# One burst per mixed step: weighted queries behind the x transpose, query transposes last, sums held back

## The chip, the cores and the metric

The kernel runs on one core of a Trainium2 chip. The metric is the device time of one execution in microseconds (us), lower is better. The engines work through instruction queues of their own: TensorE (PE, matmuls and transposes), VectorE (DVE), ScalarE (ACT), GpSimd (POOL) and SyncE (SP), which issues the DMAs. PSUM is the memory that TensorE writes, SBUF the one that holds everything else on chip.

## What is computed

Linear attention with exponential random features (8 batches, 8 heads, 576 rows, head size 64, 128 features), and a gated MLP on its result:

```python
def phi(x):                                   # x scaled by 64 ** -0.25
    h = x @ omega.T - sum(x * x) / 2          # omega: 128 x 64
    return exp(h - max(h)) / sqrt(128)
kv = phi(k).T @ v                             # 128 x 64 for a head
z = sum of phi(k) over the rows
attn = (phi(q) @ kv) / (phi(q) @ z + 1e-6)
x = attn as 4608 x 512                        # tokens x (heads * 64)
g = x @ w_gate                                # 512 x 1536
out = (g * sigmoid(g) * (x @ w_val)) @ w_out  # float32
```

The weights arrive as 64-bit numbers and are turned into float32 on the chip.

## The kernel before

**Two streams on one TensorE.** The attention runs in steps; each step takes two groups of 256 rows of two heads (a q and a k group in the mixed steps, two k groups in the first six). The MLP is a generator, `stream`, that goes over tiles of 512 tokens: gates `g` (L659, `mm1`), their Silu (L733), values `v` (L659), the product `sl` (L752) which is split in a high and a low part `hh`, `hl` (L755, L756), and the outputs `o` (L668, `mm2`). Every product is three matmuls, high by high, high by low and low by high; MLP matmuls have 512 columns. The last four tiles go in two pairs (`pair_rounds`), with seven products of combined operands in the place of eight; the sums of the products are made by `plus` (L971, DVE) and by ACT copies, the combined operands of the next pair (`t3`, `t1`, `t2`, `t4`, eight subtractions) by `next_x` (L829, DVE).

**What sets the order.** The code is recorded by the framework's list scheduler, which keeps a priority by the order of the code and puts every engine's instructions in a fixed row. The main loop calls, for each step n, the functions of a tuple in turn. `CLOSE` is for the early steps (to about 140 us), `GROUPED` for the rest: there the attention's functions stand together in a burst, and six `SHARE`s follow, each of which lets `stream` run for a share of the time that step n is given. `convert_all` (L268 to L280) turns one weight block after another into float32, one operation at a time between the shares: ACT Abs L268, DVE L270 to L278, POOL L280; in this profile it ends at about 427 us.

**A mixed step's parts.** `st_transpose` (PE `pt` L385, ACT copy `x` L393), `st_project` (PE `pp` L408, 16 matmuls), `st_max` (DVE L419 to L429), `st_exp` (ACT `ph` L440), `k_accumulate` (PE `kvacc` L542, two halves of a step, two steps later). When a half of a batch's heads is complete, `kv_finalize` copies `kvacc` to `kvr` (ACT L456).

For batches 0 to 3 a q group goes this way: `q_transpose` (PE `ptq` L566, ACT copy `qt` L568), a step later `q_mult` (PE `po` L583, eight 65-column matmuls; DVE `dn` L590, reciprocal L591, `xn` L593), a step later `q_out` (PE `xt` L616, then ACT and DVE to the MLP's `xh`, `xl`, or ACT `xo` L638 and a DMA to DRAM). For batches 4 to 7 the denominators are made before: `kv_finalize` also transposes the row of z (PE `zp` L462, ACT `zs` L464, DMA `zd` L466), `load_z` reads it back to all partitions (DMA `zt` L478), POOL multiplies (`jk` L502), DVE sums, POOL normalises `ph` (`q_norm`, L518); then `ptq` L566 and `xt` L623.

**PSUM.** `ps_moe` has three banks (`g`, `v`, `o`), `ps_proj` two (`pp`), and one bank each have `ps_tr` (`pt`, and `xt` from the mixed steps on), `kvacc`, and `ps_att`, which `po`, `ptq` and `zp` share: whoever of them comes next waits until the one before it has been read, `po` by DVE `xn`, `ptq` by ACT `qt`, `zp` by ACT `zs`.

Of the kernel before, what the change touches and what calls it, by code (L numbers as in the profile page):

```python
# [16 lines left out]
ALU = mybir.AluOpType  # L17
# [6 lines left out]
def kernel(  # L24
# [11 lines left out]
    nc = tc.nc  # L36
# [61 lines left out]
    def ps_att(name, shape):  # L98
        return ps_a.tile(shape, F32, name=name, tag="b")
# [30 lines left out]
    def slots(n, kind):  # L130

        if not 0 <= n < NS:
            return []
        return [(i, b, g, (kgroups if kd == "k" else qgroups)[g]) for i, (kd, b, g) in enumerate(steps[n]) if kd == kind]

    def pairs_of(gr):
        return [(2 * c, 2 * c + 1) for c in range(CH)] if gr is None else [gr[:1]] * CH
# [315 lines left out]
    def kv_finalize(b, a2):  # L453
        acc = kvacc.pop((b, a2))
        raw = att.tile([P, 4, VW], F32, name=f"kvr{b}_{a2}", tag="kvr", bufs=4)
        nc.scalar.copy(raw, acc)  # L456
        for j in range(2):
            kvst[b, 2 * a2 + j] = raw[:, 2 * j : 2 * j + 2, :]
        if b >= BPOOL:

            zp = ps_att(f"zp{b}_{a2}", [4, P])
            nc.tensor.transpose(zp, raw[:, :, D], ident)  # L462
            zs = att.tile([4, P], F32, name=f"zs{b}_{a2}", tag="zs")
            nc.scalar.copy(zs, zp)  # L464
            zd = dram.tile([4, P], F32, name=f"zd{b}_{a2}", tag="zd", bufs=4)
            nc.sync.dma_start(zd, zs)  # L466
            zds[b, a2] = zd

    zds = {}
    zbc = {}  # L470

    def load_z(n):

        for _, b, g, gr in slots(n, "q"):
            if g == 0 and b >= BPOOL:
                zt = att.tile([P, 2, 4, M], F32, name=f"zt{b}", tag="zt")
                for a2 in range(2):
                    nc.sync.dma_start(  # L478
                        zt[:, a2], zds.pop((b, a2)).rearrange("(o h) m -> o h m", o=1).broadcast_to([P, 4, M])
                    )  # L480
                    zbc[b, a2] = zt[:, a2]
# [42 lines left out]
    def k_accumulate(n, half):  # L524

        n -= KLAG
        ks = [(b, g, gr, c) for _, b, g, gr in slots(n, "k") for c in range(CH)]
        for b, g, gr, c in ks[half * len(ks) // 2 : (half + 1) * len(ks) // 2]:
            ph, vt = box["k", b, g], vrows[b, g]
            if c == CH - 1:  # L530
                busy.remove(vt)
                del box["k", b, g]
            for j, pr in enumerate(pairs_of(gr)[c]):
                a2 = pr // 2
                first = (b, a2) not in kvacc
                if first:
                    kvacc[b, a2] = ps_k.tile([P, 4, VW], F32, name=f"kvacc{b}_{a2}", tag="kv")
                acc = kvacc[b, a2]
                done.setdefault((b, a2), []).append(pr)
                last = LAST[pr] == (g, c)  # L540
                for hh in range(2):
                    nc.tensor.matmul(  # L542
                        acc[:, 2 * (pr % 2) + hh, :],
                        ph[:, c, hh * M : (hh + 1) * M],
                        vt[:, 2 * c + j if gr is None else c, hh, :],
                        start=first and hh == 0,
                        stop=last,
                        skip_group_check=True,
                    )
                if len(done[b, a2]) == NACC:  # L550
                    kv_finalize(b, a2)
        return bool(slots(n, "k"))
# [236 lines left out]
    sevens = {}  # L789

    factors, ahead = {}, {}

    def first_x():

# [26 lines left out]
    def next_x(r):  # L821

        for half, names in ((0, ("b11", "t1")), (1, ("b21", "b22"))):
            for j, name in zip(PAIRS[r], names):
                nc.sync.dma_start(ahead[name], x_dram[j][:, half * CH : (half + 1) * CH, :])
        yield
        for o, a, b in (("t3", "b22", "t1"), ("t1", "t1", "b11"), ("t2", "b22", "t1"), ("t4", "b21", "t2")):
            for c in range(CH):
                nc.vector.tensor_tensor(ahead[o][:, c], ahead[a][:, c], ahead[b][:, c], op=ALU.subtract)  # L829
                yield  # L830

    def new_factors():
# [5 lines left out]
    def split_x(name):  # L838
        hi, lo = factors[name]
        nc.scalar.copy(hi, ahead[name])  # L840
        nc.vector.tensor_tensor(lo, ahead[name], hi.bitcast(F32), op=ALU.subtract)
# [27 lines left out]
    def product(ps, n, wts, start):  # L869
        (wh, wl), (xh, xl) = wts[PROD[n][0]], factors[PROD[n][1]]  # L870
        for c in range(CH):
            w_ = slice(c * P, (c + 1) * P)
            for m, (a_, b_) in enumerate(((wh, xh), (wh, xl), (wl, xh))):
                nc.tensor.matmul(  # L874
                    ps, a_[:, w_], b_[:, c, :],
                    start=start and c == 0 and m == 0, stop=c == CH - 1 and m == 2, skip_group_check=True,
                )
# [6 lines left out]
    def pair_rounds(todo):  # L884
# [51 lines left out]
        for vi, (r, k_, pf) in enumerate(pair_visits):  # L936
            unit = [0]
            then = pair_visits[vi + 1] if vi + 1 < len(pair_visits) else None
            new_x = then and then[0] != r
            if k_ == 1 and r + 1 < len(PAIRS):  # L940
                prep = next_x(r + 1)
            sl, h = {}, {}

            def gate(n, src_):

                nc.scalar.activation(sl[n], src_, AF.Silu)

            def value(n, src_):

                h[n] = hbuf[used[1] % len(hbuf)]  # L950
                used[1] += 1
                hh, hl = h[n]
                nc.vector.tensor_tensor(sl[n], src_, sl[n], op=ALU.mult)
                nc.scalar.copy(hh, sl[n])
                nc.gpsimd.tensor_tensor(hl, sl[n], hh.bitcast(F32), op=ALU.subtract)

            for i, use in ((0, gate), (1, value)):
                wts = sevens[i]
                if i == 0:
                    for n in range(4):  # L960
                        sl[n] = slbuf[used[0] % len(slbuf)]
                        used[0] += 1
                keep = {}

                def copy(name, ps):
                    keep[name] = kp[:, ("m1", "m5", "u2").index(name)]
                    nc.scalar.copy(keep[name], ps)

                def plus(n, ps, name):
                    o = sl[n] if i == 0 else kp[:, 3]  # L970
                    nc.vector.tensor_tensor(o, ps, keep[name], op=ALU.add)  # L971
                    use(n, o)

                a, c, d = (ps_w.tile([P, T], F32, name=f"{e}{vi}_{i}", tag="w") for e in "acd")
                for n in ORDER:
                    weights_work(vi, unit[0])
                    unit[0] += 1
                    product({5: c, 3: c, 2: d}.get(n, a), n, wts, n in (1, 5, 2))
                    if n == 1:
                        copy("m1", a)  # L980
                    elif n == 5:
                        copy("m5", c)
                    elif n == 6:
                        copy("u2", a)
                    elif n == 3:
                        plus(1, c, "u2")
                    elif n == 7:
                        plus(3, a, "m5")
                    elif n == 2:
                        plus(0, d, "m1")  # L990
                    else:
                        use(2, a)
                    if new_x and i == 1:
                        split_x(PROD[n][1])
                    yield US7
                    if n in (5, 3, 2, 4) and one_down():
                        yield MM2
            assert not todo
            wts2 = {f: weights[f, 2] for f in (2 * pf, 2 * pf + 1)}
            for j, o in ((PAIRS[r][1], 1), (PAIRS[r][0], 0)):  # L1000
                ht = {2 * pf + n: h[2 * n + o] for n in range(2)}
                todo += [(j, k_, ht, wts2, None, tt) for tt in range(T // P)]
# [7 lines left out]
    def give(us):  # L1010
# [28 lines left out]
    )  # L1039
    GROUPED = (  # L1040
        q_out,
        st_project,
        q_transpose,
        lambda n: k_accumulate(n, 0),
        lambda n: k_accumulate(n, 1),
        st_max,
        st_exp,
        q_den,
# [2 lines left out]
        SHARE,  # L1051
        SHARE,
        lambda n: q_norm(n + 1),
        q_mult,
        SHARE,
        SHARE,
        SHARE,
# [68 lines left out]
```

## Time and profile before

| | |
|---|---|
| time, median of 3 runs | 1218.34 us (1216.60 to 1220.92) |
| the profiled execution | 1219.54 us, of it span 1217.8 us, 1.7 us around it |
| PE busy, share of the span | 1173.9 us, 96% |
| ACT, DVE, POOL busy | 54%, 53%, 48% |
| mean granted TensorE clock | 0.987 of full speed |
| PE busy in 100 to 200, 200 to 300, 300 to 400, 400 to 500 us | 95.7, 95.6, 96.3, 94.5 |
| PE busy in 600 to 800, 800 to 900, 900 to 1000 us | 199.95, 94.3, 100 |
| DVE busy in 100 to 200, 200 to 300 us | 83.8, 50.8 |

Profile times count from the start of the span. A row of the timeline has start, duration, engine, line, operation, output and inputs, their shapes and the count of merged instructions; brackets hold the idle time of the engine ahead of it and what released it. MLP matmuls start 0.227 us apart at full clock, though the modelled duration shown is 0.39: spacing is what counts. A row of the waits has the total, the times and the longest.

### The profile page before, as it was taken

The numbers are of one execution on the slowest core, as the hardware profiler recorded it, in microseconds if no ns is written. First come the engines' busy times: TensorE is split into PE (matmuls) and PEld (weight loads), VectorE is DVE, ScalarE is ACT, GpSimd is POOL, SyncE is SP. The second block draws the span as 40 slices with busy tenths as digits, with TensorE's granted clock in tenths as the row PEclk, the third lists the DMA queues.
The fourth block names the chain that finished last, engine by engine and source line by source line (L and its number), as shares of the span: only waits on it lengthen the run. The fifth ranks groups of instructions, "written<-read, shape, count | busy, mean of one in ns | idle before, by whom it ended". The sixth has DMA issues, their size and how long they took to land.

```text
span 1217.8 us, 18846 instructions
## 1 busy us (share of the span) xinstructions
PE 1173.9 (96%) x6705; PEld 969.5 (80%) x6705; DVE 647.1 (53%) x1231; ACT 660.9 (54%) x1461; POOL 585.0 (48%) x500
## 2 busy tenths in 40 slices
PE   6999999999999999999999999999899999999998
PEld 5888887888787678878888877878688888888886
DVE  5588886364656763434333354174545456545544
ACT  4687866574465555466555666353454445454431
POOL 3343442254344645545454585444565553555541
PEclk9799999999999999999999999999999999999999
DMA  6556656253544433244222211334321111312103
GB/s 151 125 132 157 168 146 186 50 153 86 170 113 119 119 86 93 71 112 101 66 62 81 67 60 45 88 103 138 96 55 58 48 49 26 104 52 53 52 18 69
DMA packets 174109, 113.52 MB, mean 93 GB/s; under 512 B 125856, under 2 KB 144320, under 8 KB 174016
## 3 DMA queue, kind: packets, MB, share of 16 engines
q1 hardware_dynamic: 174016, 112.32, 34.1%
q8 instruction: 53, 0.87, 0.3%
q14 instruction: 40, 0.33, 0.1%
HBM read 87.10 MB, written 25.18 MB: 92 GB/s over the span
## 4 chain that ended last, share of the span: by engine, by line
PE 78%; DVE 8%; DMA 5%; POOL 3%; issue 3%; ACT 2%; SPq 1%; POOLq 0%; ACTq 0%; DVEq 0%
PE o L668 21%; PE g L659 11%; PE a L874 10%; PE v L659 10%; PE pp L408 5%; PE c L874 5%; PE kvacc L542 4%; PE ptq L566 3%; PE d L874 2%; PE pt L385 2%; DMA nat<-in_k_dram 2%; PE po L583 2%; PE xt L623 1%; DVE st L426 1%; SPq L343 1%
## 5 line engine op out<-in xcount | busy, mean ns | idle before, releaser
L440 ACT ACTIVATE ph<-pp,st 128x128 f32<-128x128 f32 x576 | 157.5, 390 | 32.8 <-DVE st L429 32.3
L697 DVE TENSOR_TENSOR acc<-o,acc 128x512 f32<-128x512 f32 x140 | 95.8, 685 | 100.5 <-PE o L668 100.3
L392 POOL TENSOR_TENSOR sq<-nat 128x512 f32<-128x512 f32 x72 | 77.2, 1072 | 120.1 <-DMA nat<-in_k_dram 98.7
L426 DVE TENSOR_REDUCE st<-pp 128x4 f32<-128x512 f32 x144 | 93.0, 683 | 68.0 <-PE pp L408 67.9
L251 POOL TENSOR_TENSOR wlo<-wraw,whi 128x512 fp32r<-128x512 f32 x76 | 99.9, 1325 | 55.5 <-ACT whi L250 55.2
L408 PE MATMUL pp<-omT,x 64*128 64x128 f32 x1152 | 97.4, 301 | 5.5 <-ACT x L393 4.5
L668 PE MATMUL o<-whi,hh 128*128 128x512 f32 x240 | 96.6, 402 | 6.3 <-ACT sl L733 3.4
L408 PEld LDWEIGHTS pp<-omT,x 64*128 64x128 f32 x1152 | 79.4, 199 | 24.1 <-issue 11.6
L756 POOL TENSOR_TENSOR hl<-sl,hh 128x512 fp32r<-128x512 f32 x60 | 78.8, 1318 | 37.5 <-ACT hh L755 37.4
L659 PE MATMUL g<-xh,whi 128*128 128x512 f32 x240 | 96.9, 404 | 0.0
L659 PE MATMUL v<-xh,whi 128*128 128x512 f32 x240 | 95.7, 399 | 0.7 <-DVE acc L697 0.7
L668 PE MATMUL o<-whi,hl 128*128 128x512 f32 x240 | 94.4, 393 | 0.9 <-POOL hl L756 0.9
L659 PE MATMUL g<-xl,whi 128*128 128x512 f32 x240 | 94.4, 393 | 0.0
L659 PE MATMUL g<-xh,wlo 128*128 128x512 f32 x240 | 94.4, 393 | 0.0
L668 PE MATMUL o<-wlo,hh 128*128 128x512 f32 x240 | 94.3, 393 | 0.0
L659 PE MATMUL v<-xh,wlo 128*128 128x512 f32 x240 | 93.7, 391 | 0.0
L659 PE MATMUL v<-xl,whi 128*128 128x512 f32 x240 | 93.6, 390 | 0.0
L502 POOL TENSOR_TENSOR jk<-ph,zt 128x512 f32<-128x512 f32 x32 | 41.3, 1295 | 107.0 <-ACT ph L440 106.9
L280 POOL TENSOR_TENSOR wc<-st,wc 128x512 f32<-128x512 f32 x36 | 48.7, 1355 | 90.4 <-DVE wc L278 43.8
L419 DVE TENSOR_REDUCE st<-sq 128x8 f32<-128x512 f32 x72 | 49.0, 681 | 80.6 <-POOL sq L392 80.6
L865 POOL TENSOR_TENSOR wlo<-s,whi 128x512 fp32r<-128x512 f32 x44 | 65.2, 1498 | 33.9 <-DVE late L971 12.1
L865 POOL TENSOR_TENSOR wlo<-wraw,whi 128x256 fp32r<-128x256 f32 (+1 forms) x44 | 45.6, 1036 | 72.9 <-ACT whi L864 72.3
(252 smaller groups left out, 2925.3 us busy)
## 6 DMA issues: line engine op xcount, KB each, us to landing
wraw<-wscr SPq DMA_DIRECT2D x120, 256.0 KB, 2.7
wscr<-wc SPq DMA_DIRECT2D x36, 256.0 KB, 2.4
out_dram<-acc SPq DMA_DIRECT2D x72, 128.0 KB, 2.3
nat<-in_k_dram SPq DMA_DIRECT2D x64, 128.0 KB, 2.9
v<-in_v_dram SPq DMA_DIRECT2D x64, 128.0 KB, 3.3
nat<-in_q_dram SPq DMA_DIRECT2D x64, 128.0 KB, 2.9
st<-in_moe_w_gate_dram SPq DMA_DIRECT2D x12, 512.0 KB, 4.4
st<-in_moe_w_val_dram SPq DMA_DIRECT2D x12, 512.0 KB, 4.9
```

Of the source, the lines that this page charges most:

```text
L251: nc.gpsimd.tensor_tensor(lo, raw, hi.bitcast(F32), op=ALU.subtract)
L392: nc.gpsimd.tensor_tensor(sq, nat, nat, op=ALU.mult)
L408: nc.tensor.matmul(pp[hh][:, i, c, :], x[r, i, c * P : (c + 1) * P], omT[r], start=True, stop=True)
L419: nc.vector.tensor_reduce(st[:, 0].rearrange("p i c h -> p (i c h)"), sq.rearrange("p i c h d -> p (i c h) d"), axis=AX.X, op=ALU.add,)
L426: nc.vector.tensor_reduce(st[:, 1, :, :, hh], pp[hh], axis=AX.X, op=ALU.max, negate=True)
L440: nc.scalar.activation(ph[:, c, hh * M : (hh + 1) * M], pp[hh][:, i, c, :], AF.Exp, bias=st[:, 3, i, c, hh : hh + 1], scale=1.0,)
L659: nc.tensor.matmul(ps, a_[:, ws], b_[:, c, :], start=n == 0, stop=n == 3 * NC - 1)
L668: nc.tensor.matmul(ps, a_[:, ts_], b_, start=first and n == 0, stop=last and n == 2)
L697: nc.vector.tensor_tensor(a_, po, a_, op=ALU.add)
L756: nc.gpsimd.tensor_tensor(hl, h, hh.bitcast(F32), op=ALU.subtract)
L865: nc.gpsimd.tensor_tensor(lo, src_, hi.bitcast(F32), op=ALU.subtract)
L874: nc.tensor.matmul(ps, a_[:, w_], b_[:, c, :], start=start and c == 0 and m == 0, stop=c == CH - 1 and m == 2, skip_group_check=True,)
```

## The change

Three edits. In `GROUPED`, `q_mult` moves from between the shares to directly behind `q_out`, and `q_transpose` behind both `k_accumulate`. `kv_finalize` no longer transposes z; it lists the halves, and `z_rows` does it a step later, behind `st_project` (or in `load_z` at the latest). And `next_x`'s subtractions carry an ordering dependency, without a semaphore, on the latest sum that `plus` made.

```diff
--- before.py
+++ after.py
@@ -457,7 +457,12 @@
         for j in range(2):
             kvst[b, 2 * a2 + j] = raw[:, 2 * j : 2 * j + 2, :]
         if b >= BPOOL:
-
+            z_todo.append((b, a2, raw))
+
+    def z_rows(_):
+
+        while z_todo:
+            b, a2, raw = z_todo.pop(0)
             zp = ps_att(f"zp{b}_{a2}", [4, P])
             nc.tensor.transpose(zp, raw[:, :, D], ident)
             zs = att.tile([4, P], F32, name=f"zs{b}_{a2}", tag="zs")
@@ -466,6 +471,7 @@
             nc.sync.dma_start(zd, zs)
             zds[b, a2] = zd
 
+    z_todo = []
     zds = {}
     zbc = {}
 
@@ -473,6 +479,7 @@
 
         for _, b, g, gr in slots(n, "q"):
             if g == 0 and b >= BPOOL:
+                z_rows(n)
                 zt = att.tile([P, 2, 4, M], F32, name=f"zt{b}", tag="zt")
                 for a2 in range(2):
                     nc.sync.dma_start(
@@ -789,6 +796,7 @@
     sevens = {}
 
     factors, ahead = {}, {}
+    latest = [None]
 
     def first_x():
 
@@ -826,7 +834,14 @@
         yield
         for o, a, b in (("t3", "b22", "t1"), ("t1", "t1", "b11"), ("t2", "b22", "t1"), ("t4", "b21", "t2")):
             for c in range(CH):
-                nc.vector.tensor_tensor(ahead[o][:, c], ahead[a][:, c], ahead[b][:, c], op=ALU.subtract)
+                sub = nc.vector.tensor_tensor(ahead[o][:, c], ahead[a][:, c], ahead[b][:, c], op=ALU.subtract)
+
+                tc.add_manual_dep(
+                    sub.ins,
+                    latest[0].ins.name,
+                    mybir.DependencyInfo(mybir.DependencyClass.NoSync, mybir.DependencyReason.DATA),
+                    reason="TensorE waits for the products' sums, nothing waits for these",
+                )
                 yield
 
     def new_factors():
@@ -968,7 +983,7 @@
 
                 def plus(n, ps, name):
                     o = sl[n] if i == 0 else kp[:, 3]
-                    nc.vector.tensor_tensor(o, ps, keep[name], op=ALU.add)
+                    latest[0] = nc.vector.tensor_tensor(o, ps, keep[name], op=ALU.add)
                     use(n, o)
 
                 a, c, d = (ps_w.tile([P, T], F32, name=f"{e}{vi}_{i}", tag="w") for e in "acd")
@@ -1039,10 +1054,12 @@
     )
     GROUPED = (
         q_out,
+        q_mult,
         st_project,
-        q_transpose,
+        z_rows,
         lambda n: k_accumulate(n, 0),
         lambda n: k_accumulate(n, 1),
+        q_transpose,
         st_max,
         st_exp,
         q_den,
@@ -1051,7 +1068,6 @@
         SHARE,
         SHARE,
         lambda n: q_norm(n + 1),
-        q_mult,
         SHARE,
         SHARE,
         SHARE,
```

The first place is PE's row around step 36, at a batch's end (names carry the step, or the buffer; `pp` are the projections, `kvacc` k's sums, `g`, `v`, `o` the MLP). Before, with the MLP's 24 matmuls between `kvacc_1` and `po` left out:

```order
L616 MATMUL xt_0_3167<-ident,xn_0_3130 128x128 x2
...
L408 MATMUL pp_36_3174<-omT,x_3064 128x128
L566 MATMUL ptq_2_3183<-ident,ph_35_3049 128x128 x4
L542 MATMUL kvacc_0_2641<-vrest_105,ph_34_2893 128x65 x4
L385 MATMUL pt_3222<-ident,nat_2850 128x128 x4
L462 MATMUL zp_0_3196<-ident,kvr_0_3194 4x128
L542 MATMUL kvacc_1_3202<-vrest_105,ph_34_2893 128x65 x4
...
L583 MATMUL po_1_3264<-kvr_0_2062,qt_1_3038 128x65 x4
```

The same after:

```order
L623 MATMUL xt_0_3167<-ident,xn_0_3031 128x128 x2
L590 MATMUL po_1_3173<-kvr_0_2065,qt_1_3052 128x65 x4
...
L408 MATMUL pp_36_3184<-omT,x_3074 128x128
L549 MATMUL kvacc_0_2644<-vrest_105,ph_34_2907 128x65 x4
L573 MATMUL ptq_2_3204<-ident,ph_35_3059 128x128 x4
L549 MATMUL kvacc_1_3199<-vrest_105,ph_34_2907 128x65 x4
L385 MATMUL pt_3226<-ident,nat_2850 128x128 x4
```

`po` stands in the burst, ahead of `ptq` and in the same bank; `zp` has left it.

The second place is step 46, where the first half of a later batch is complete. ACT's row before (`hh` is the MLP's high part, `xo` the attention's result, `ph` the exponentials):

```order
L755 CAST hh_7_4615<-sl_7_4421 128x512
L638 COPY xo_1_4_4640<-xt_1_4637 128x256
L755 CAST hh_8_4696<-sl_8_4423 128x512
L568 COPY qt_2_4658<-ptq_2_4653 128x512
L268 ACTIVATE wc_0_4850<-st_0_4717 128x512
L440 ACTIVATE ph_46_4669<-pp_46_4643,st_4538 128x128 x2
```

and after:

```order
L762 CAST hh_7_4609<-sl_7_4421 128x512
L645 COPY xo_1_4_4634<-xt_1_4631 128x256
L762 CAST hh_8_4696<-sl_8_4423 128x512
L469 COPY zs_0_4649<-zp_0_4647 4x128
L575 COPY qt_2_4662<-ptq_2_4657 128x512
L440 ACTIVATE ph_46_4669<-pp_46_4637,st_4532 128x128 x2
```

`zs` now stands behind `hh_8`. PE's row there, after the change:

```order
L408 MATMUL pp_46_4638<-omT,x_4531 128x128
L467 MATMUL zp_0_4647<-ident,kvr_0_4491 4x128
L549 MATMUL kvacc_1_4493<-v_101,ph_44_4381 128x65 x4
L573 MATMUL ptq_2_4657<-ident,ph_44_4376 128x128 x4
L385 MATMUL pt_4685<-ident,nat_4340 128x128 x4
```

`ptq` follows `zp` in the bank that `zs` empties.

The third place is DVE's row in the first pair round, where the next pair's operands are made (`late` are buffers of `next_x` and of the kept sums, `s` the combined weights). Before:

```order
L853 TENSOR_TENSOR s_0_0_9249<-wraw_0_9200,s_0_0_9249 128x256
L829 TENSOR_TENSOR late_8878<-late_8877,late_8876 128x512 x2
L829 TENSOR_TENSOR late_8876<-late_8876 128x512 x2
L971 TENSOR_TENSOR sl0k<-c_0_9105,late_8880 128x512
L829 TENSOR_TENSOR late_8877<-late_8877,late_8876 128x512 x2
L829 TENSOR_TENSOR late_8879<-late_8878,late_8877 128x512 x2
L971 TENSOR_TENSOR sl2k<-a_0_9104,late_8880 128x512
L971 TENSOR_TENSOR late_8879<-d_0_9106,late_8880 128x512
```

and after:

```order
L868 TENSOR_TENSOR s_0_0_9249<-wraw_0_9200,s_0_0_9249 128x256
L986 TENSOR_TENSOR sl0k<-c_0_9105,late_8880 128x512
L837 TENSOR_TENSOR late_8878<-late_8877,late_8876 128x512
L986 TENSOR_TENSOR sl2k<-a_0_9104,late_8880 128x512
L986 TENSOR_TENSOR late_8879<-d_0_9106,late_8880 128x512
L837 TENSOR_TENSOR late_8878<-late_8877,late_8876 128x512
L837 TENSOR_TENSOR late_8876<-late_8876 128x512 x2
```

One subtraction, not eight, stands ahead of the sum `sl2k`.

## The prediction

> **What bounds the kernel now.** I read the page's busy shares first, then its chain, then what TensorE waited for, then the stretches of the timeline that the three edits touch.
>
> ```profile
> span 1217.8 us, 18846 instructions
> PE 1173.9 (96%) x6705; PEld 969.5 (80%) x6705; DVE 647.1 (53%) x1231; ACT 660.9 (54%) x1461; POOL 585.0 (48%) x500
> PE 78%; DVE 8%; DMA 5%; POOL 3%; issue 3%; ACT 2%; SPq 1%; POOLq 0%; ACTq 0%; DVEq 0%
> ```
>
> TensorE is the bound: it is busy 96% of the span and holds 78% of the chain. The other engines matter only where TensorE stops for them, so everything that the change can give or take is in TensorE's waits, in the spacing of its matmuls, and in the clock that it is granted after a stop. No matmul of the MLP goes away. The waits that the edits touch, over the whole span (total, times, longest):
>
> ```profile
> PE xt L616 <- DVE xn L593: 5.2, 8, 1.1
> PE a L874 <- DVE sl2k L971: 3.2, 1, 3.2
> PE pt L385 <- ACT xo L638: 2.5, 1, 2.5
> ```
>
> The first belongs to the burst, the second to the held back sums; the third is not touched and serves below for the clock. The first one again, between 180 and 420 us alone:
>
> ```profile
> PE xt L616 <- DVE xn L593: 4.0, 5, 1.1
> ```
>
> So 4.0 us of it lie in the steps that the new order covers. The rest of 1.2 is earlier, where the other tuple rules.
>
> **Term A, `po` joins the burst.** A switch between the MLP's 512-column matmuls and small ones costs TensorE something. Alone between MLP matmuls, and eight matmuls of the same shape inside a burst:
>
> ```profile
> 300.94 0.40 PE L659 MATMUL g<-xh,wlo 128*128 128x512 f32 x1
> 301.18 1.00 PE L583 MATMUL po<-kvr,qt 128*128 128x65 f32 x8
> 301.99 0.48 PE L659 MATMUL g<-xh,whi 128*128 128x512 f32 x1
> 302.30 0.39 PE L659 MATMUL g<-xl,whi 128*128 128x512 f32 x1
> ...
> 338.94 1.00 PE L542 MATMUL kvacc<-v,ph 128*128 128x65 f32 x8
> 339.78 0.61 PE L385 MATMUL pt<-ident,nat 128*128 128x128 f32 x4
> ```
>
> From 300.94 to 302.30 are 1.36 us for two MLP matmuls (0.45) and `po`: `po` costs 0.91 alone. In a burst its like costs 339.78 - 338.94 = 0.84. That is 0.07 for each of some 18 mixed steps with a `po`: -1.2 us. Bounds: 0 (the burst's other switches absorb it) and -1.8 (0.10 each).
>
> **Term B, `xn` against `ptq`.** With `po` a step earlier, `xn` is long done when `xt` wants it, so the 4.0 us go. But `ptq` now follows `po` in the one bank that they share, and waits until DVE has read it. Where DVE is free:
>
> ```profile
> 231.86 1.00 PE L583 MATMUL po<-kvr,qt 128*128 128x65 f32 x8
> ...
> 233.31 0.42 DVE L593 TENSOR_TENSOR xn<-po,dn 128x256 f32<-128x256 f32 x1
> ```
>
> The bank is read 1.87 us after `po` starts (233.73). TensorE needs 0.84 for `po`, 1.09 for `pp` and 0.84 for `kvacc`, 2.77 in all, before it reaches `ptq`: no wait. Where DVE is behind, `xn` is too. How late it is there shows from the first `pp` matmul to the first reduction that reads it:
>
> ```profile
> 263.20 1.16 PE L408 MATMUL pp<-omT,x 64*128 64x128 f32 x16
> 266.57 1.28 DVE L426 TENSOR_REDUCE st<-pp 128x4 f32<-128x512 f32 x2
> ...
> 308.82 1.16 PE L408 MATMUL pp<-omT,x 64*128 64x128 f32 x16
> 313.75 1.28 DVE L426 TENSOR_REDUCE st<-pp 128x4 f32<-128x512 f32 x2
> ```
>
> That is 3.37 and 4.93 here; in the same rows of the other steps with a `ptq` behind a `po` 3.51 (at 170.10), 3.04 (192.62), 3.32 (292.81), and 1.2 to 2.5 elsewhere. In the new row DVE's three small operations stand directly ahead of that reduction, and the 0.83 us that they take there they no longer take earlier; so `xn` ends where the reduction now begins, and `ptq` waits for the lateness less 2.77: 0.74 + 0.27 + 0.60 + 0.55 + 2.16 = 4.3 us. The first mixed step of the new kind pays once more: its `po` has `qt` just ahead, an ACT copy of 0.58 (term D's rows), +0.6. B = -4.0 + 4.3 + 0.6 = +0.9. Bounds: -4.0, if DVE keeps up, and +5, if in each of the five one more conversion operation (0.4 to 1.3 long) gets ahead of `xn`.
>
> **Term C, the sums held back.**
>
> ```profile
> 877.03 1.28 DVE L829 TENSOR_TENSOR late<-late,late 128x512 f32<-128x512 f32 x2
> 878.24 1.29 DVE L829 TENSOR_TENSOR late<-late 128x512 f32<-128x512 f32 x2
> 879.44 0.69 DVE L971 TENSOR_TENSOR sl0k<-c,late 128x512 f32<-128x512 f32 x1
> 880.04 2.49 DVE L829 TENSOR_TENSOR late<-late,late 128x512 f32<-128x512 f32 x4
> 882.45 0.69 DVE L971 TENSOR_TENSOR sl2k<-a,late 128x512 f32<-128x512 f32 x1
> ...
> 879.59 0.39 PE L668 MATMUL o<-whi,hl1k 128*128 128x512 f32 x1
> 883.19 0.80 PE L874 MATMUL a<-t4hi,whi 128*128 128x512 f32 x1 [3.21 <-DVE sl2k L971]
> 885.91 0.48 PE L668 MATMUL o<-whi,hh0k 128*128 128x512 f32 x1
> ```
>
> Product 4 cannot start in `a`'s bank before `sl2k` has read it, and seven of eight subtractions stand ahead. In the new row one does: from 877.03 DVE makes `sl0k`, one subtraction and `sl2k` in 3 x 0.60 + 0.1, done by 878.95, ahead of 879.82 when TensorE wants the bank. The six matmuls then end by 881.18 (879.82 + 6 x 0.227), where before the next began at 885.91: 4.7 us. Of it 3.4 are the wait and 1.3 the slow matmuls behind it, 0.43 us apart. What is late next: the Silu and casts of `sl0k` on ACT and the split on POOL, wanted by TensorE only with the next product and the next outputs; the seven subtractions left over run in DVE's gaps, which was busy only 53 of 100 us there. C = -4.7; bounds -5.0 and -3.4 (the clock falls for another reason), and 0 in a rival.
>
> The clock, in stretches with TensorE's busy time and granted clock:
>
> ```profile
> 203.40:206.80 3.40, 3.40 (x21) 2.86 (x22) 1.50 (x4) 0.53 (x2) 1.86 (x2) 0.51 0.97 292
> 387.80:391.20 3.40, 2.42 (x11) 1.76 (x13) 1.80 (x6) 0.00 (x0) 1.04 (x1) 1.00 0.00 0
> 456.00:459.40 3.40, 3.40 (x10) 2.63 (x9) 0.00 (x0) 3.38 (x9) 0.88 (x1) 0.50 0.74 190
> 882.70:886.10 3.40, 2.91 (x7) 2.36 (x8) 1.03 (x2) 2.15 (x5) 3.40 (x3) 0.50 0.24 77
> ```
>
> A stop of 3.2 us, one of 2.5 (the `pt` wait) and two of 1.05 close together (at 203) were each followed by a stretch at half clock; a loss of some 1.7 us at most. After about 1.3 us idle the clock stayed at 1.00 (387.80). [...]
>
> **Term D, z's transposes leave the end of the burst.** Before, `zp` followed `pt` and waited for its own `kvr` copy:
>
> ```profile
> 394.06 0.60 PE L385 MATMUL pt<-ident,nat 128*128 128x128 f32 x4
> 394.69 0.27 PE L462 MATMUL zp<-ident,kvr 128*4 128x128 f32 x1
> 394.80 1.00 PE L542 MATMUL kvacc<-vrest,ph 128*128 128x65 f32 x8
> ```
>
> `pt` to `zp` takes 0.63 where `pt` to the next matmul took 0.36 at 339.78 (an MLP matmul at 340.14): 0.27 for four of the eight `zp`, about -1.0. Bounds 0 and -2 (all eight). SP's `zd` and `zt` go past one step's loads of q, k and v; POOL's products, which read `zt`, come a step or more after, so nothing waits.
>
> At step 46 the move costs. `ptq` now needs the bank of `zp`, and `zs` stands on ACT behind a cast that waits for DVE:
>
> ```profile
> 412.99 0.62 ACT L755 CAST hh<-sl 128x512 fp32r<-128x512 f32 x1 [3.79 <-DVE sl L752]
> 413.51 0.58 ACT L568 COPY qt<-ptq 128x512 f32<-128x512 f32 x1
> ...
> 409.25 0.66 PE L385 MATMUL pt<-ident,nat 128*128 128x128 f32 x4
> 409.67 0.48 PE L659 MATMUL g<-xh,whi 128*128 128x512 f32 x1
> ...
> 420.92 0.50 PE L668 MATMUL o<-whi,hh 128*128 128x512 f32 x1 [2.82 <-ACT sl L733]
> ```
>
> TensorE would be at `ptq` at about 408.65; `zs` comes at 413.5 and takes 0.3: a new wait of 5.2 us. But later TensorE stopped 2.82 us for the Silu anyway, which ACT still reaches at about 421. The gates, begun at 414.8 in the place of 409.67, end at 423.1; the outputs begin then, not at 420.92: +2.2. The half-clock stretch behind the 2.82 goes and one behind the new wait comes. D2 = +2.2; bounds 0 (DVE makes that `sl` earlier) and +5.2 (the Silu is pushed back too).
>
> **The sum.** A -1.2, B +0.9, C -4.7, D -1.0, D2 +2.2: -3.8 us. The profiled execution took 1219.54, 1.2 above the median of 1218.34, so by it 1215.7, by the median 1214.5; I say 1214.6. A measurement of this kernel can tell about 0.3% (3.7 us): faster is below 1214.7, slower above 1222.0.
>
> **The rivals.**
> 1. *DVE keeps up.* The waits for `xn` go and none for `ptq` comes; the half clock at 203, which two such stops made, goes with them. For it: the free case above has 0.9 us to spare. Against: the five late steps. Time: -1.2 - 4.0 - 1.7 - 4.7 - 1.0 + 2.2 = -10.4, 1207.9.
> 2. *Slower: `ptq` behind `xn` in one bank.* With `po` in the burst, DVE's lateness lands on TensorE in the same step, where before a step's work lay between. It decides once DVE is more than 2.8 us behind at a burst; five steps are. If the conversion operations get ahead, the five waits grow by 1 us each, and three of them (over 1.5 to 2 us) halve the clock for 1.7 us each: -3.8 + 5 + 5.1 = +6.3, 1224.6. [...]
> 3. *The hold-back does not deliver*: another wait (the DMA of weights, POOL's split) ends in the same place. Then C is 0 and the sum +0.9: 1219.2. Against: nothing else in the rows around 879 is later than 879.8.
>
> **How the numbers follow.** The forecast's case 0.47, with its own range 1211 to 1219; DVE keeps up 0.22; the bank 0.20; no delivery 0.11. Faster: half of the first, and the second: 0.24 + 0.22 = 0.46. Slower: most of the bank's case, 0.17, and 0.02 of the others: 0.19. The rest is 0.35. The range reaches from the fast rival to the lower half of the slow one, 1208 to 1223.
>
> **What would show it.** In the changed profile: no wait of `xt` for `xn` after 180 us; waits of `ptq` for `xn` at the five steps, 4 us together; no stop before product 4 near 880 and clock 1.00 behind it; a stop of `ptq` for `zs` near 410 with the outputs 2 us later. Wrong would be: waits of `ptq` far above 4 us, a half clock behind them, or the stop at 880 under another name.

## The result, and the profile after

The changed kernel takes 1237.15 us (median of 4 runs, 1234.39 to 1237.99) against 1217.8 for the kernel before (median of 4, 1216.6 to 1220.92): ratio 1.0151, 95% interval 1.0125 to 1.0177. It is slower by some 18 us, where 4 us faster was forecast. The profiled execution is the fastest of the changed kernel's runs (1234.39).

From its page, the span, the busy times and the chain, then the rows of what TensorE waited for (total, times, longest):

```profile
span 1232.3 us, 18853 instructions
PE 1176.9 (95%) x6705; PEld 976.9 (79%) x6705; DVE 650.7 (53%) x1231; ACT 659.0 (53%) x1461; POOL 586.4 (48%) x500
PE 73%; DVE 7%; DMA 7%; POOL 4%; ACT 3%; issue 3%; SPq 2%; POOLq 0%; ACTq 0%; DVEq 0%
...
PE ptq L573 <- DVE xn L600: 13.4, 9, 3.5
PE o L675 <- DVE acc L704: 7.0, 1, 7.0
PE ptq L573 <- ACT zs L469: 6.1, 1, 6.1
PE a L889 <- ACT late L982: 3.4, 3, 1.9
PE xt L623 <- DVE xn L600: 1.2, 3, 0.8
```

The work is the same and the busy times hardly moved. The waits of `xt` for `xn` are down from 5.2 to 1.2 us and the one of product 4 for `sl2k` is gone, as forecast. In their place stand 13.4 us of `ptq` for `xn`, 6.1 of `ptq` for `zs`, 7.0 of `o` for `acc`, DVE's addition that empties the bank of `o` (2.3 at its longest before), and a new 1.95 of product `a` for ACT's copy `late`.

**Where the time went.** The MLP's matmuls come in the same sequence in all these kernels, but for three near 223 us. So I took the start of the same matmul in each profile, less its start in the profile of before, and formed the difference over each stage. In us, by the times of before (the kernels other than the changed one, `after`, are those of the experiments below):

| stage | after | order | zmove | hold | banks | banksj | hold2 | mended |
|---|---|---|---|---|---|---|---|---|
| 137 to 260 | +3.3 | +0.9 | +1.1 | +2.5 | -1.0 | -0.1 | +2.3 | +0.7 |
| 260 to 299 | +10.6 | +6.9 | -0.0 | +0.2 | -1.1 | -1.2 | +0.1 | -1.1 |
| 299 to 380 | -2.0 | -1.5 | -0.1 | +0.1 | -2.5 | -2.5 | -0.1 | -1.8 |
| 380 to 399 | +6.9 | +6.8 | +0.1 | +1.7 | +6.3 | +2.3 | +0.1 | +2.4 |
| 399 to 474 | +1.2 | +2.2 | -2.3 | +0.6 | +2.9 | +0.9 | +0.2 | +3.9 |
| 474 to 856 | -0.5 | -0.1 | -1.4 | -1.1 | -0.7 | -1.4 | -0.9 | -0.0 |
| 856 to 887 | -4.9 | -0.1 | +0.2 | -4.7 | -4.7 | -4.8 | -4.7 | -5.0 |
| 887 to 910 | +2.2 | +0.3 | +0.0 | +3.8 | +3.8 | +3.8 | +0.0 | -0.0 |

The table is of one profile for each kernel. `hold` and `hold2` have before's order up to some 850 us, and yet +2.5 and +2.3 ahead of 260: that much is chance. Ahead of 137 us the profiles differ by -8 to +2 us, and I draw nothing from that stretch (the profiled run of `order`, 1226.88, is the fastest of its seven, median 1237.39, and 8 us of that lie there). The changed kernel's 16.8 us behind 137 are the bursts up to 299, the stop at 388, and then a gain at 880 of which half is given back.

**A burst.** TensorE and DVE at step 36 of the changed kernel:

```profile
263.37 1.00 PE L590 MATMUL po<-kvr,qt 128*128 128x65 f32 x8
270.04 1.09 PE L573 MATMUL ptq<-ident,ph 128*128 128x128 f32 x4 [3.54 <-DVE xn L600]
...
263.36 1.52 DVE L270 TENSOR_SCALAR wc<-wc 128x512 f32<-128x512 f32 x1
268.46 0.69 DVE L278 SCALAR_TENSOR_TENSOR wc<-st,wc 128x512 f32<-128x512 uint32 x1
269.47 0.42 DVE L600 TENSOR_TENSOR xn<-po,dn 128x256 f32<-128x256 f32 x1
```

and the stretch behind the stop, with TensorE's busy time and, third from the end, its granted clock:

```profile
271.80:275.20 3.40, 3.40 (x14) 3.07 (x14) 0.00 (x0) 3.39 (x10) 0.00 (x0) 0.54 0.83 233
```

`po` is done by 264.3, but DVE has a whole conversion of weights ahead (263.36 to 269.1), and `xn` frees the bank at 269.9. TensorE stands 3.54 us, and the next stretch runs at 0.54 of the clock: 5.8 us for this one burst, 0.8 of it `po` itself, which came back as -0.9 where it had stood alone. Step 38 is the same again (3.35 us at 304.03). Between 137 and 380 us TensorE's clock was at half from 206.7 to 210.1, 268.1 to 274.9 and 302.2 to 309.0; before, only from 203.4 to 206.8.

**The stop for `acc`,** a chain through four engines, in the order of its links:

```profile
386.03 0.69 DVE L513 TENSOR_REDUCE dj<-jk 128x4 f32<-128x512 f32 x1 [1.59 <-POOL jk L509]
386.63 0.64 DVE L276 TENSOR_SCALAR wc<-st 128x512 int32<-128x512 int32 x1
391.06 1.30 POOL L280 TENSOR_TENSOR wc<-st,wc 128x512 f32<-128x512 f32 x1
392.38 0.32 SPq L283 DMA_DIRECT2D wscr<-wc  x1
397.67 0.65 SPq L343 DMA_DIRECT2D nat<-in_k_dram  x1
400.71 1.04 POOL L392 TENSOR_TENSOR sq<-nat 128x512 f32<-128x512 f32 x1 [5.58 <-DMA nat<-in_k_dram]
402.45 0.68 DVE L704 TENSOR_TENSOR acc<-o,acc 128x512 f32<-128x512 f32 x1
403.19 0.80 PE L675 MATMUL o<-whi,hh 128*128 128x512 f32 x1 [7.04 <-DVE acc L704]
```

One late thing passes through four queues. DVE's conversion step L276 stands behind `dj`; POOL's last conversion step ends at 392.4; SP issues the store at 392.38, and the loads of q, k and v, which stand behind it in SP's row, from 396.01 to 397.67; the squares of that k come at 401.75; and the MLP's addition, which stands behind their reduction on DVE, lets TensorE go. The same links in the profile before, with the same k group:

```profile
374.20 1.32 POOL L280 TENSOR_TENSOR wc<-st,wc 128x512 f32<-128x512 f32 x1 [2.79 <-issue]
375.55 0.32 SPq L283 DMA_DIRECT2D wscr<-wc  x1
382.68 0.64 SPq L343 DMA_DIRECT2D nat<-in_k_dram  x1
```

The store left 16.8 us later than before, while TensorE was 9.7 late at that point; the load of k 15.0 later.

### The profile page after: what moved, and what is told of

Read it like the earlier page. It is cut to its first block, busy times and chain, and to the rows that moved or that the text cites. A ratio compares the mean times of both kernels' runs of the same rounds, so it can differ in the third digit from the quotient of the medians.

```text
span 1232.3 us, 18853 instructions
## 1 busy us (share of the span) xinstructions
PE 1176.9 (95%) x6705; PEld 976.9 (79%) x6705; DVE 650.7 (53%) x1231; ACT 659.0 (53%) x1461; POOL 586.4 (48%) x500
## 4 chain that ended last, share of the span: by engine, by line
PE 73%; DVE 7%; DMA 7%; POOL 4%; ACT 3%; issue 3%; SPq 2%; POOLq 0%; ACTq 0%; DVEq 0%
PE o L675 21%; PE a L889 10%; PE g L666 9%; PE v L666 8%; PE c L889 5%; PE pp L408 5%; PE kvacc L549 4%; PE d L889 3%; DMA nat<-in_k_dram 3%; PE ptq L573 2%; PE pt L385 2%; PE po L590 1%; PE xt L630 1%; DMA st<-in_moe_w_val_dram 1%; DMA st<-in_moe_w_gate_dram 1%
## 5 line engine op out<-in xcount | busy, mean ns | idle before, releaser
L880 POOL TENSOR_TENSOR wlo<-s,whi 128x512 fp32r<-128x512 f32 x44 | 66.3, 1522 | 34.4 <-DVE late L986 11.9
```

What stands on the lines that cost most here:

```text
L880: nc.gpsimd.tensor_tensor(lo, src_, hi.bitcast(F32), op=ALU.subtract)
```

## The experiments

All are timed in 5 rounds beside the kernel before on the same chip.

**1. The three edits one by one.** `hold` is the kernel before with the edit in `next_x` and `plus` alone, `zmove` with `z_rows` alone, `order` with this alone:

```diff
     GROUPED = (
         q_out,
+        q_mult,
         st_project,
-        q_transpose,
         lambda n: k_accumulate(n, 0),
         lambda n: k_accumulate(n, 1),
+        q_transpose,
...
-        q_mult,
```

> The kernel before with the new order of po and ptq alone: z's transposes stay in kv_finalize and nothing is held back. If the shared bank of po and ptq is the cause, ptq waits for xn 10 us or more in all between 170 and 380 us, two or three half-clock stretches follow, and the time is 8 to 13 us above before: 1226 to 1231. If z's move is what made DVE and ACT late, it is within 3 us of before.

> The kernel before with z's transposes a step later alone; po and ptq stand where they stood, nothing is held back. If the stop of ptq for zs near 410 to 430 us belongs to this edit alone, it is there with 5 to 6 us, some 2 to 3 of it come back at the stop for the Silu behind it, and the time is 2 to 6 us above before: 1220 to 1224. If that stop needs the other order as well (DVE late from the bursts), within 1 us of before.

> The kernel before with the hold-back of the next pair's subtractions alone. If that edit is worth what the two traces show around 880 us (the offset between them falls by some 5 us there and 2 come back at a stop of product a for the late buffer's copy), it is 3 to 5 us faster than before: 1213 to 1215. If the gain at 880 is only moved to another stop, within 1 us of before. The stop at 880 is gone under both.

Measured, ratio to before: `order` 1.0147 (1.0125 to 1.0168), `zmove` 1.0000 (0.9976 to 1.0024), `hold` 0.9984 (0.9953 to 1.0014). The new order of `po` and `ptq` alone makes the whole slowdown; the expected 8 to 13 us were too few (some 18). The other two edits are worth nothing that these runs can tell; `hold` was expected 3 to 5 us faster. TensorE's waits in `order`, then in `zmove`, then in `hold`:

```profile
PE ptq L566 <- DVE xn L593: 8.8, 6, 3.5
PE o L668 <- DVE acc L697: 6.8, 1, 6.8
PE zp L462 <- DVE xn L593: 2.7, 1, 2.7
```

```profile
PE ptq L573 <- ACT zs L469: 4.3, 2, 4.0
```

```profile
PE a L882 <- ACT late L975: 3.5, 3, 1.9
```

In `order`, the stop for `acc` is there with no z moved. In `zmove` the stop for `zs` is there, but what stood behind it shrinks: +5.3 us to 413, then -7.6 to 474. So it nets about -2, not +2 to +6 as expected: the stop of 2.82 us for the Silu, which stood behind it before, is gone.

**2. `banks`: `ptq` in one of the MLP's three banks**, in the changed kernel.

```diff
-            pt = (ps_moe if m < EARLY else ps_tr if i else ps_att)(f"ptq{b}_{g}", [P, 2, G])
+            pt = ps_moe(f"ptq{b}_{g}", [P, 2, G])
```

> The changed kernel with ptq in one of the three MLP banks in place of the bank that po and zp use; all else is the change. If the one bank is the cause, the waits of ptq for xn and zs go, and with them 13 + 6 us and their half-clock stretches: 1212 to 1220. If DVE's lateness itself is the cause, TensorE stops for the same time at the next thing that DVE or ACT owe (pp for ph, o for acc, or g for its bank): 1230 or more.

Ratio 1.0031 (1.0008 to 1.0054). One bank's name takes back some 14 of the 18 us, which leaves the time just above the 1212 to 1220 expected for this cause and far below the 1230 of the other. No wait of `ptq` for `xn` or `zs` is left, and the stages between 260 and 380 us are 3.6 us *faster* than before. DVE is nearly as late as in the changed kernel: its `xn` at step 36 ends 5.7 us after `po`'s start (6.5 there).

```profile
258.05 1.00 PE L590 MATMUL po<-kvr,qt 128*128 128x65 f32 x8
263.35 0.42 DVE L600 TENSOR_TENSOR xn<-po,dn 128x256 f32<-128x256 f32 x1
```

So most of the lateness is not made by the waits; it costs only where TensorE needs what DVE holds. What stays is the stop for `acc`, with 7.0 us as in the changed kernel.

**3. `order2`: `po` last in the burst,** behind `ptq` and both halves of k's sums; the kernel before otherwise.

```diff
     GROUPED = (
         q_out,
         st_project,
         q_transpose,
         lambda n: k_accumulate(n, 0),
         lambda n: k_accumulate(n, 1),
+        q_mult,
...
-        q_mult,
```

> The kernel before with po moved to the end of the burst, behind ptq and both halves of k's sums, and ptq where it was. po then waits for the ACT copy of ptq, and the next user of their bank comes a step later. If the order of the two in the bank is what cost, ptq waits for nothing, the waits of xt for xn are gone too, and the time is within 4 us of before, rather below (0.997 to 1.0). If joining the burst is bad in itself, because DVE and ACT are late there whatever stands first, TensorE waits 8 us or more for qt or xn and the ratio is 1.007 or more.

Ratio 1.0097 (1.0059 to 1.0135): the first theory fails in this form. With the order turned round, the bank waits for ACT in the place of DVE, as the longest of TensorE's waits shows, and then the rows of ACT and TensorE at step 38:

```profile
PE po L583 <- ACT qt L568: 6.8, 7, 2.9
```

```profile
301.86 0.62 ACT L755 CAST hh<-sl 128x512 fp32r<-128x512 f32 x1 [3.22 <-DVE sl L752]
302.39 0.58 ACT L568 COPY qt<-ptq 128x512 f32<-128x512 f32 x1
303.02 1.97 PE L583 MATMUL po<-kvr,qt 128*128 128x65 f32 x8 [2.93 <-ACT qt L568]
```

`ptq` was done at 299.0; its copy stood behind a cast that waited for DVE's conversion. So the two users of the bank wait for each other through whichever engine is behind, in either order: 8.8 us for DVE in `order`, 6.8 for ACT here.

**4. `banksq`: the store of converted weights on POOL's own queue,** on top of `banks`.

```diff
-            nc.sync.dma_start(wscr[f, i], u)
+            nc.gpsimd.dma_start(wscr[f, i], u)
```

> The changed kernel with ptq in an MLP bank, as before, and the store of the converted weights (wscr) issued by GpSimd's queue in place of SP's, so that SP no longer stands behind POOL's last operation of a conversion. If the stop of o for acc near 388 to 400 us comes from SP (the store waits for POOL, the loads of k behind it come late, the squares, the reduction and acc's addition behind them), it falls from 7 to some 2 us or below and the ratio to before from 1.003 to about 0.999. If DVE's own order (a conversion step behind the sum of jk) makes it, the stop stays at 6 us or more.

Ratio 1.0153 (1.0116 to 1.0189), and the stop grew. The test does not tell SP from DVE. SP now has no store to issue, but its load of the stored weights (`wraw`), which stands ahead of the loads of k, left 4.58 us after the store (393.84 to 398.42; 2.26 in the changed kernel, 392.38 to 394.64), and the stores from POOL's queue landed later: a median of 4.4 us from issue to landing, where SP's took 2.5 in `banks`. TensorE's wait, the rows of the two queues at the stop, and the landing times (first `banksq`, then `banks`):

```profile
PE o L675 <- DVE acc L704: 12.6, 3, 9.3
```

```profile
393.84 0.59 POOL L283 DMA_DIRECT2D wscr<-wc  x1 [0.30 <-POOL wc L280]
398.42 0.32 SPq L308 DMA_DIRECT2D wraw<-wscr  x1
```

```profile
wscr<-wc POOLq DMA_DIRECT2D x36, 256.0 KB, 4.4
wscr<-wc SPq DMA_DIRECT2D x36, 256.0 KB, 2.5
```

**5. `banksj` and `afterj`: a buffer of its own for `xn`.** `xn` and `jk` share two buffers. With `po` a burst earlier, `xn` of the last group of batch 3 is made ahead of `jk` of the first group of batch 4, so `jk` now waits until an `xn` has been transposed; behind `jk` stand the normalising, the conversion's last step on POOL, and `dj` on DVE. `banksj` has this edit on top of `banks`, `afterj` on the changed kernel alone.

```diff
-            xn = att.tile([P, CH, 2, D], F32, name=f"xn{b}_{g}", tag="jx")
+            xn = att.tile([P, CH, 2, D], F32, name=f"xn{b}_{g}", tag="xn", bufs=1)
```

POOL's row at step 43 in `banks`, where `jk_0` and `jk_1` stand ahead of the conversion `wc_0`, and in `banksj`:

```order
L509 TENSOR_TENSOR jk_0_4250<-ph_42_4086,zt_4191 128x512
L280 TENSOR_TENSOR wc_2_4337<-st_2_4187,wc_2_4337 128x512
L525 TENSOR_TENSOR ph_42_4086<-ph_42_4086,dj_0_4252 128x512
L509 TENSOR_TENSOR jk_1_4386<-ph_43_4240,zt_4191 128x512
...
L525 TENSOR_TENSOR ph_43_4240<-ph_43_4240,dj_1_4388 128x512
L280 TENSOR_TENSOR wc_0_4452<-st_0_4335,wc_0_4452 128x512
```

```order
L509 TENSOR_TENSOR jk_0_4250<-ph_42_4086,zt_4191 128x512
L525 TENSOR_TENSOR ph_42_4086<-ph_42_4086,dj_0_4252 128x512
...
L280 TENSOR_TENSOR wc_2_4337<-st_2_4187,wc_2_4337 128x512
L509 TENSOR_TENSOR jk_1_4386<-ph_43_4240,zt_4191 128x512
L280 TENSOR_TENSOR wc_0_4452<-st_0_4335,wc_0_4452 128x512
```

> The changed kernel with ptq in an MLP bank and, further, a buffer of its own for xn, which shares two buffers with jk in all kernels so far. If the stop of o for acc near 388 to 400 us comes from that sharing (jk of the first later batch now waits for an xn made a burst earlier, the normalising and the conversion of weights behind it on POOL and DVE come late, then SP's loads of k), the stop falls from 7 us to 2.5 or below and the time by some 4 us against ptq's bank alone: ratio to before 0.999 or below. If the loads of k are late for another reason, the stop stays at 6 to 7 us and the ratio at 1.003.

> The changed kernel with a buffer of its own for xn alone; ptq stays in po's bank. If the two causes are independent, the stop for acc goes (4 to 5 us) and the waits of ptq for xn and zs stay at 15 us or more: ratio to before about 1.011. If the shared buffers also made DVE late at the earlier bursts, the waits of ptq fall too and the ratio is 1.005 or less.

`banksj` 1.0012 (0.9981 to 1.0042), `afterj` 1.0090 (1.0058 to 1.0122). The stop for `acc` falls from 7.0 to 3.2 us in both (2.5 or below was expected of `banksj`, and a ratio of 0.999 or below; before, it was 2.3), and the stage 380 to 399 from +6.3 to +2.3 in the one and +6.9 to +2.3 in the other. That the shared buffers make most of this stop is shown by the profiles; the ratios alone (1.0031 against 1.0012) overlap. In `afterj` the waits for the bank stay, so they do not come from the shared buffers:

```profile
PE ptq L573 <- DVE xn L600: 14.4, 8, 3.4
PE ptq L573 <- ACT zs L469: 6.0, 1, 6.0
PE o L675 <- DVE acc L704: 3.2, 1, 3.2
```

**6. `hold2`: the subtractions behind the products of the values too.** In `hold` the stop near 906 us ate most of the gain. DVE, POOL, ACT and TensorE there:

```profile
899.20 3.49 DVE L830 TENSOR_TENSOR late<-late,late 128x512 f32<-128x512 f32 x2
902.62 0.68 DVE L961 TENSOR_TENSOR sl1k<-a,sl1k 128x512 f32<-128x512 f32 x1
...
900.39 1.75 POOL L963 TENSOR_TENSOR hl0k<-late,hh0k 128x512 fp32r<-128x512 f32 x1
...
903.33 0.62 ACT L962 CAST hh1k<-sl1k 128x512 fp32r<-128x512 f32 x1 [2.56 <-DVE sl1k L961]
904.85 0.58 ACT L975 COPY late<-a 128x512 f32<-128x512 f32 x1
...
905.49 0.50 PE L882 MATMUL a<-t2hi,whi 128*128 128x512 f32 x1 [1.95 <-ACT late L975]
```

Two of the subtractions that were held back stand ahead of `sl1k`, and beside POOL they take some 1.75 us each. ACT's cast waits for `sl1k`, the copy of `a` stands three places behind that cast, and TensorE wants `a`'s bank. The mend:

```diff
-                nc.vector.tensor_tensor(sl[n], src_, sl[n], op=ALU.mult)
+                latest[0] = nc.vector.tensor_tensor(sl[n], src_, sl[n], op=ALU.mult)
```

> The kernel before with the hold-back alone, but the subtractions ordered also behind the latest product of the values (L953 before), where the first form put two of them ahead of the product that ACT, and then TensorE's product a, waited for. If those two subtractions are the cause of the stop near 906 us, that stop is gone with its 3.9 us, the stop at 880 stays gone, and the time is 4 to 6 us below before: 0.995 to 0.997. If the stop near 906 has another cause (ACT's own row, the weights' DMA), it stays and the ratio is 0.998 to 1.0.

Ratio 0.9949 (0.9925 to 0.9973): some 6 us faster than before, and faster than the changed kernel. Both stops are gone; product 4 follows the outputs 0.22 us after:

```profile
879.85 0.39 PE L668 MATMUL o<-whi,hl1k 128*128 128x512 f32 x1
880.07 0.39 PE L882 MATMUL a<-t4hi,whi 128*128 128x512 f32 x1
```

**7. Combinations.** `best` is `order2` with `hold2`'s edit.

> Both: po at the end of the burst, and the subtractions held back behind sums and products. If the two are independent, the sum of their differences: 0.992 to 0.997.

1.0074 (1.0049 to 1.0098), a miss: 0.0023 below `order2` but slower than before; the joined burst spoils it. `best3` has `hold2`, the new order with `ptq` in an MLP bank and `xn` in its own buffer, and z's transposes where they were before.

> po behind x's transpose and ptq last in the burst, but ptq in an MLP bank, xn in a buffer of its own, z's transposes where they were before, and the subtractions held back behind sums and products. If both causes are removed, the burst's gain (some 4 us between 140 and 380 us in the run with ptq's bank) adds to the 6 us of the hold-back: ratio to before 0.990 to 0.994. If the burst's gain is given back elsewhere, 0.995, as with the hold-back alone.

1.0084 (1.0054 to 1.0114), a miss. Its own new wait, from TensorE's waits:

```profile
PE zp L462 <- DVE xn L593: 4.3, 2, 2.2
```

`zp` still shares the bank with `po`, and at the end of the burst it waits for `xn` as `ptq` did. Its longest stop, 4.11 us of `pt` for ACT's `xo` at 439.01, stands where `mended` has one of 3.30 and the kernel before none. The rest of its excess I did not trace. `mended` is the whole change with the three edits of `banks`, `banksj` and `hold2`.

> The whole change with its three troubles mended: ptq in an MLP bank, xn in a buffer of its own, the subtractions held back behind the products of the values too. If the three are independent of each other, it is 3.9 us (the stop near 906 us) faster than the kernel with the first two: ratio to before about 0.998. If the burst then is worth what its stages between 137 and 380 us showed (3 to 4 us), it matches the mended hold-back alone at 0.995; if the stops for xo and the Silu between 400 and 440 us stay, it is 0.997 to 0.999.

0.9979 (0.9956 to 1.0003). That is the change as far as it can be mended here: it is not shown to be faster than before, nor better than `hold2` alone (0.9949). The gain at the bursts is given back between 380 and 474 us (+2.4 and +3.9 in the table), where TensorE stops 3.31 us for `acc` (2.32 before) and 3.30 for ACT's `xo` at 429.19, a stop that the kernel before does not have and `order` has with 2.67. The stop for the Silu (2.69) was there before (2.82). Why `xo` is late there was not tried.

## Why the prediction was wrong, by its own steps

**Term B failed.** It took DVE's lateness at a burst as fixed and subtracted 2.77. In the new kernel DVE is later: at step 36 `xn` ends 6.5 us after the burst reaches `po` (263.37 to 269.89), where I had 3.37. Of these 3.1 us more, 2.4 show at the head of DVE's row. The reduction of squares there began 3.6 us ahead of the burst before the change (`pp` at 263.20) and 1.2 ahead of it now:

```profile
259.62 0.69 DVE L419 TENSOR_REDUCE st<-sq 128x8 f32<-128x512 f32 x1 [2.77 <-POOL sq L392]
...
262.16 0.69 DVE L419 TENSOR_REDUCE st<-sq 128x8 f32<-128x512 f32 x1 [3.56 <-POOL sq L392]
```

Measured from the same MLP matmul (at 258.25 before, 260.21 now), TensorE reaches the burst 1.8 us sooner than before, mostly since `po` no longer stands ahead of it (0.9) and `xt` no longer waits there (0.55); the reduction itself is 0.6 late. So most of the 2.4 comes from the prediction's own gains: they bring TensorE sooner to a DVE that is no faster. In `banks` TensorE is sooner by the same 1.8 and the reduction is not late, 2.05 us ahead. Another 0.5 are slower conversion steps (1.52 and 1.37 against 1.28 and 1.15). What made the load under that reduction 0.6 late was not tried and stays open. So the five waits that I put at 4.3 us were nine with 13.4. Then the clock fell behind the stops (0.54 behind the 3.54 us above), which B left out of its sum though the same text had shown the clock to do so. (Two readings there were loose: the stop behind which the clock stayed at 1.00 was 2.32 us long, spread over two stretches with 2.06 and 2.42 of 3.40 us busy, and of the two stops at 203 only one was for `xn`, the other for ACT's `ph`.) B and A together were forecast at -0.3 us; the stages 137 to 380 show +11.9. The rival "`ptq` behind `xn` in one bank" had the mechanism and the place, with a chance of 0.20. Its price for A and B, +9.8 us, was near the +11.9; its time of 1224.6 was still 12.6 short of 1237.15, among other things because it had no stop for `acc`.

**A link that no term had: the shared buffers.** The stop for `acc` cost 6.9 us, of which a buffer of its own for `xn` took back 4.0 to 4.6. I followed the bank that `po` and `ptq` share and the queues that they pass, but not the two SBUF buffers that `xn` shares with `jk`. The order of after showed the conversion behind `dj` at that step, and I did not look there.

**Term C was right in size and missed its sequel.** 4.9 us came at 880 (4.7 forecast). The sentence that POOL's split and ACT's casts would be wanted only later looked one product ahead; the seven subtractions that were left did not run in gaps, and 2.2 us (3.8 in `hold`) went at 906.

**Term D and D2.** The first half of z at the burst of 266 us gave nothing (-0.0 in `zmove`, -0.27 forecast). D2's stop came as forecast, at the same place and nearly the same size:

```profile
430.55 0.62 ACT L762 CAST hh<-sl 128x512 fp32r<-128x512 f32 x1 [4.08 <-DVE sl L759]
431.08 0.25 ACT L469 COPY zs<-zp 4x128 f32<-4x128 f32 x1
431.47 0.87 PE L573 MATMUL ptq<-ident,ph 128*128 128x128 f32 x3 [6.08 <-ACT zs L469]
```

6.08 us (5.2 forecast). Its net price did not come as forecast (+2.2): z moved alone makes the stages 399 to 474 2.3 us faster (`zmove`), and the +1.2 of the changed kernel there is 1.0 less than the +2.2 of `order`, which moves no z. D2 took 3.0 us off for the later stop for the Silu; the shrinkage behind the new stop was 7.6 in `zmove`. ACT keeps its order there: `zs` runs 6.8 us behind its `zp` (424.29 to 431.08), directly behind the cast that waited 4.08 us.

**Term A** held. At step 36 `xt` to `pp` takes 1.15 us with `po` between them (263.16 to 264.31) and 0.34 before, so `po` costs 0.81 in the burst, and 0.9 come back where it had stood alone: -0.1 a step (-0.07 forecast). The stages 260 to 380 of `banks` are 3.6 us faster than before, with the 2.1 us of waits for `xn` of that stretch and A's gain in one.

## What to carry to other kernels

Before work is put together in one burst, list every buffer that it shares, in PSUM and in SBUF, and for each the engine that frees it: here the burst waited 8.8 us for DVE with `po` ahead of `ptq` (`order`) and 6.8 us for ACT with the order turned round (`order2`). Lateness of another engine is not a constant that can be read off the old profile: at step 36 DVE stood 2.4 us further behind TensorE at the head of its row, most of it because TensorE came 1.8 us sooner, and the changed kernel also moved the loads and reductions that stand ahead (one load of k left 15.0 us later). Work that is held back has to land somewhere: follow it past everything that it now stands ahead of, not only past what it made late.

## What the runs showed of the hardware

DVE's subtraction of two SBUF operands of 128x512 takes 0.68 us alone (894.92 in the changed kernel, with POOL idle) and some 1.75 beside POOL (3.49 for the two at 899.20 in `hold`). POOL's own instruction there, at 900.39, takes 1.75 too, where the same line takes 1.30 at 894.03.

A DMA that POOL issued cost it 0.59 us in `banksq` and landed 4.4 us after its issue (median of 36), where SP's took 2.5 in `banks`; with the 36 issues on POOL the kernel went from 1.0031 to 1.0153.
